# Last output rows by single PSUM banks on three DMA queues, with a new order of all steps

## The chip, the cores and the metric

The kernel runs on one core of a Trainium2 chip. The metric is device time in microseconds; a kernel's time is the median of its runs. The core's engines are TensorE (PE, with its weight loads as PEld), VectorE (DVE), ScalarE (ACT), GpSimd (POOL) and SyncE (SP). Each works through its own instructions in order and waits on semaphores of the others. TensorE writes to PSUM, whose eight banks hold 512 float32 values per partition; ScalarE and VectorE empty them. Transfers run on 16 shared DMA engines and are issued here from POOL (loads) and SP (transposes, output).

## The reference: linear attention into a gated long convolution

For 8 batches of 576 positions, 8 heads of 64 make a model width of 512. All inputs and the output are float32.

```python
kv  = einsum('bhsd,bhse->bhde', k, v)
out = einsum('bhsd,bhde->bhse', q, kv)
out = out / sqrt(mean(out * out, -1) + 1e-6) * g_norm
x   = out.transpose(0, 2, 1, 3).reshape(8, 576, 512)

x1, x2, x3 = split(x @ w_proj, 3, axis=-1)           # w_proj is 512 x 1536
conv = irfft(rfft(x2, axis=1) * rfft(filter, axis=0))   # circular, length 576
return (x1 * conv * x3) @ w_out                       # 512 x 512
```

## The kernel before: a written-out order of small steps

Matrix products run in bfloat16 with float32 sums. The program is one long list of steps, `ORDER`. A word such as `Ga2.0` names a step (`Ga2`) and its batch (0). The loop at the end calls the steps one after another, each of which appends its instructions to the queues of the engines. Nothing is planned at run time: `ORDER` alone decides what stands ahead of what on each engine. A third number, as in `T0.0.19`, asks for so many *fillers* before the step: matmuls of `nil` by `ind`, constants made at the start, into the PSUM bank that the step has just taken. Their results are never read. `take` hands out PSUM banks by the order too, a pair or a single bank, the longest free first.

The names of the steps, by batch:

- `Lq`, `Lk`, `Lv` (halves with `a`, `b`) load q, k, v from POOL's queue, cast to bfloat16 on the way; `Lf` loads the filter, `Lw1`, `Lw2`, `Lw3` the thirds of w_proj, `Lwo` w_out.
- `T0`, `T1` with `eT…` transpose q on TensorE (batches 0 and 1; later `Qt`, by DMA, with `Qh`).
- `K` multiplies k by v, `eK` copies the result; `O` multiplies by q; `sq`, `R`, `rs`, `ob` or `ov`, `x` make the normalisation (square, sum over a head, reciprocal root, scale by g, product).
- `eo`, `fr`, `fa` fold x; `rrM`, `rrT`, `abM`, `abT` project the folded rows to x2; `err`, `eab`, `eT` evict; `F0`, `F1t`, `F1`, `F2c`, `F2` transform; `M0`, `M1`, `M2` multiply with the filter's spectrum; `A0`, `A1` add on POOL (`Av0`, `Av1` on VectorE).
- `Io`, `I` transform back, `oa`, `ov`, `ea`, `ev` evict (a on ScalarE, v on VectorE); `vB`, `w` recombine, `fin` (or `f0`, `f1` by halves) multiplies with the gates.
- `Ga`, `Gb` project to x1 and x3 for one of four column groups; `x1j` (or `xv`) evicts the first, `g` multiplies the second with it.
- `U0`, `U2` multiply two groups of 128 rows with w_out into two banks, `U4` one group that joins the end of an even batch and the begin of the next; `ot…` evicts on ScalarE and sends from SP's queue. `V0` to `V3` do one group of 128 rows into one bank; `va`, `vv` evict and `ds`, `dg` send. `send` cuts a tile at multiples of 96 rows, so a group of 128 rows goes out as two transfers.
- At the start, `Z…` steps make constants, `Ad`, `As`, `Ab`, `Ac` the cosine and sine tables, `Tb`, `et`, `ec` transpose them; `Rv`, `er`, `ff`, `H`, `hv`, `hs`, `Hv`/`HN` make the filter's spectrum.

The start runs: loads on POOL; on TensorE 19 fillers, then q's transposes, more fillers, tables, filter, K.0, O.0 and the first gates (`Ga2.0`). The end runs: the gates of batch 7, the last inverse transforms, the last recombination on VectorE, then `U2.6`, `U2.7`, `V0.7`, `V1.7`, `U4.7` on TensorE, evictions on ScalarE, and sends on SP with one on POOL.

Of the kernel before, what the change touches and what calls it, by code (L numbers as in the profile page):

```python
# [23 lines left out]
sq3.0 ob3.0 Lw2.0 R3.0 hs0.0 x0.0 hv2.0 rs3.0 R2.0 T1.1 rs2.0 ob2.0 x1.0 T0.1 eTa0.1 Lkb.2 Lq.2 hs2.0 Ga2.0.1 Ga3.0
Gb2.0 eTa1.1 Hv1.0 Gb3.0 eo.0 fr.0 x13.0 x12.0 Lq.3 Lka.2 K.1 eK.1 g2.0 Ga1.0 O01.1 g3.0 HN0.0 sq0.1 rrM.0 Lv.2 x11.0
fa1.0 rrT.0 sq1.1 ob1.1 fa0.0 ob0.1 verr.0 abM.0 eab.0 F0.0 abT.0.1 F2c.0 eT.0 O23.1 M0.0 F2.0 sq2.1 Gb1.0 ob2.1 sq3.1
F1t.0 M2.0 A0.0 F1.0 Qt.3 g1.0 ob3.1 R1.1 Ga0.0.1 rs1.1 M1.0 Av1.0 R0.1 R2.1 rs0.1 rs2.1 R3.1 Gb0.0 rs3.1 x.1 Io01.0
eo.1 x10.0 Io23.0 oa01.0 K.2 I01.0 oa23.0 ea01.0 Ga1.1 fr.1 eK.2 Ga0.1 x11.1 Qt.2 I23.0 rrM.1 g0.0 ea23.0 rrT.1 x10.1
err.1 fa.1 O01.2 sq0.2 abT.1 abM.1 sq1.2 vB.0 w.0 ob0.2 f001.0 ob1.2 f101.0 veT.1 eab.1 Gb1.1 O23.2 sq2.2 F0.1 g1.1
ob2.2 Qh.3 Ga3.1 f123.0 f023.0 Gb0.1 sq3.2 ob3.2 R1.2 x13.1 F2c.1 M0.1 rs1.2 g0.1 F2.1 Lk.3 R3.2 F1t.1 rs3.2 Lv.3 R2.2  # L30
rs2.2 M2.1 F1.1 K.3 eK.3 Lqb.4 M1.1 R0.2 Lwo.0 Ga2.1 rs0.2 Gb2.1 O23.3 x12.1 x.2 sq2.3 g2.1 Av1.1 Lv.4 U0.0 sq3.3 R3.3
Lqa.4 Lka.4 Lkb.4 A0.1 ob2.3 eo.2 ob3.3 Gb3.1 Lq.5 rs3.3 ot0.0 I01.1 ea01.1 g3.1 fa0.2 Ga0.2 x10.2 Io23.1 Io01.1
oa23.1 fa1.2 abT.2 I23.1 oa01.1 eT.2 ea23.1 O01.3 fr.2 sq1.3 abM.2 sq0.3 ob1.3 vB.1 Qt.5 w.1 Qt.4 rrM.2 rrT.2 fin.1
eab.2 F1t.2 err.2 K.4 F1.2 Ga3.2 eK.4 ob0.3 x13.2 Gb0.2 R1.3 Gb3.2 rs1.3 M1.2 F0.2 R2.3 g0.2 Ga2.2 g3.2 R0.3 rs2.3
Ga1.2 x12.2 M0.2 rs0.3 x11.2 U4.1 F2c.2 O23.4 A1.2 F2.2 ot4.1 x.3 sq3.4 ob3.4 M2.2 Av0.2 sq2.4 U2.0 ob2.4 Gb2.2 Io01.2
I23.2 ot2.0 g2.2 oa01.2 eo0.3 eo1.3 fa0.3 Qh.5 I01.2 ea23.2 Io23.2 ea01.2 fr.3 R3.4 U0.1 Gb1.2 rs3.4 oa23.2 fa1.3
ot0.1 g1.2 O01.4 sq0.4 vB.2 abT.3 sq1.4 abM.3 Lk.5 eT.3 Lv.5 Lq.6 ob0.4 Lv.6 rrM.3 w.2 f023.2 rrT.3 eab.3 ob1.4 f001.2
F2c.3 K.5 F1t.3 F2.3 F1.3 verr.3 eK.5 R2.4 Ga1.3 Lk.6 M2.3 U2.1 rs2.4 M1.3 f123.2 x11.3 F0.3 ot2.1 R0.4 Ga2.3 rs0.4
R1.4 x12.3 Gb2.3 M0.3 rs1.4 g2.3 x.4 Lv.7 Ga0.3 O23.5 x10.3 sq2.5 sq3.5 ob3.5 f101.2 Gb1.3 U0.2 ob2.5 g1.3 ot0.2 Ga3.3
x13.3 Av0.3 Qt.6 A1.3 eo.4 I01.3 fa0.4 fa1.4 Io23.3 Io01.3 oa23.3 Gb3.3 ea01.3 g3.3 fr.4 I23.3 K.6 oa01.3 O01.5 ea23.3  # L40
eK.6 sq1.5 sq0.5 Gb0.3 g0.3 ob1.5 ob0.5 abM.4 R2.5 rrM.4 vB.3 w001.3 w101.3 abT.4 w023.3 w123.3 fin.3 eab.4 rs2.5 Qh.6
R1.5 eT.4 rrT.4 F1t.4 rs1.5 err.4 F1.4 R0.5 Ga2.4 rs0.5 x12.4 M1.4 Gb2.4 R3.5 F0.4 A1.4 g2.4 Lk.7 rs3.5 M0.4 U2.2 x.5
U4a.3 U4b.3 A0.4 O23.6 F2c.4 ot2.2 F2.4 sq3.6 ot4.3 sq2.6 ov3.6 M2.4 U0.3 eo.5 Ga0.4 ob2.6 ot0.3 I01.4 x10.4 Io01.4
oa01.4 fr.5 Io23.4 oa23.4 Ga3.4 ev01.4 I23.4 ea23.4 x13.4 Lqa.7 Lqb.7 Qt.7 Qh.7 Gb3.4 vB01.4 rrM.5 O01.6 g3.4 sq1.6
vB23.4 ob1.6 rrT.5 verr.5 Gb0.4 g0.4 Ga1.4 x11.4 Gb1.4 R3.6 Ga1.5 sq0.6 ob0.6 fa.5 R2.6 g1.4 rs3.6 F0.5 w.4 rs2.6
abT.5 eT.5 abM.5 x11.5 fin.4 eab.5 M0.5 R1.6 Gb1.5 rs1.6 K.7 F1t.5 g1.5 F2c.5 eKv.7 F2.5 M2.5 R0.6 F1.5 A0.5 rs0.6
M1.5 U2.3 ot2.3 Ga3.5 A1.5 x13.5 Gb3.5 O23.7 x.6 U0.4 sq2.7 g3.5 sq3.7 ov3.7 eo.6 Ga0.5 ob2.7 ot0.4 I23.5 Io23.5 x10.5
Io01.5 Gb0.5 ov23.5 oa01.5 ev23.5 I01.5 ea01.5 fa.6 g0.5 R2.7 Ga2.5 rs2.7 x12.5 abM.6 vB.5 abT.6 O01.7 eab.6 eT.6
Gb2.5 sq0.7 ob0.7 fr.6 w.5 rrM.6 sq1.7 g2.5 rrT.6 fin.5 F2c.6 ob1.7 F1t.6 F2.6 R1.7 err.6 M2.6 F1.6 U0.5 rs1.7 ot0.5
F0.6 Ga1.6 M1.6 R3.7 U2.5 x11.6 R0.7 M0.6 rs3.7 Ga2.6 U2.4 Av0.6 rs0.7 x0.7 A1.6 ot2.5 Gb2.6 x1.7 Io01.6 x12.6 eo.7  # L50
Gb1.6 g2.6 ot2.4 g1.6 Ga0.6 Io23.6 Gb0.6 oa01.6 oa23.6 I23.6 x10.6 I01.6 fa.7 ea23.6 ea01.6 abM.7 abT.7 Ga3.6 fr1.7
g0.6 eab.7 fr0.7 Gb3.6 vB.6 w.6 eT.7 rrM.7 x13.6 F2c.7 g3.6 rrT.7 F1t.7 F1.7 Ga0.7 err.7 fin.6 F2.7 F0.7 U4.5 M1.7
Ga1.7 x10.7 U0.6 x11.7 Gb1.7 M0.7 ot0.6 M2.7 Gb0.7 ot4.5 g1.7 A1.7 A0.7 g0.7 I01.7 Io01.7 Ga2.7 Io23.7 oa01.7 ev01.7
I23.7 oa23.7 Gb2.7 ea23.7 x12.7 Ga3.7 Gb3.7 vB01.7 vB23.7 g2.7 U2.6 w101.7 x13.7 ot2.6 g3.7 f101.7 w123.7 f123.7 U2.7
w023.7 ot2.7 w001.7 f023.7 f001.7 V0.7 V1a.7 V1b.7 U4.7 va1.7 va0.7 ds0.7 va4.7 dg1.7 ds4.7"""


@with_exitstack
def kernel(
# [697 lines left out]

    def send(q, b, at, ot):  # L760

        for i, x in enumerate([ot] if len(ot.shape) == 2 else [ot[:, 0], ot[:, 1]]):
            at_, p = at + i * P, 0
            while p < P:
# [1 line left out]
                q.dma_start(out=o_rows(b, at_ + p, n), in_=x[p:p + n])
                p += n

    def o_rows(b, at, n):
        b, a, c, p = b + at // S, at % S // TH, at % TH // 96, at % 96  # L770
        return bass.AP(tensor=out.tensor, offset=out.offset + (b * S + 6 * p + 2 * c + a) * DM, ap=[[6 * DM, n], [1, DM]])
# [11 lines left out]
            for dc in range(NDC):  # L783
                nc.tensor.matmul(pp[:, cc], ygt(b)[:, dc, b % 2 * 64 + c * P:b % 2 * 64 + (c + 1) * P], wo[:, dc], start=(dc == 0), stop=(dc == NDC - 1))  # L784

    def U_ev(b, c0, ev=act.copy):
        ot = ot_tile()
        ev(out=ot, in_=tmp['u', b, c0])  # L788
        free(("u", b, c0))
        send(nc.sync, b, b % 2 * 64 + c0 * P, ot)  # L790

    def U4(b, d0, d1):
# [2 lines left out]
        for dc in range(d0, d1):  # L795
            nc.tensor.matmul(tmp['u4', b], yg4()[:, b // 2 % 2, dc, 4 * P:5 * P], wo[:, dc], start=(dc == 0), stop=(dc == NDC - 1))
# [13 lines left out]
    step["ot4"] = U4_ev  # L810
    step["ov4r"] = lambda b: U4_ev(b, vec.tensor_copy)


# [12 lines left out]
        ev(out=ot, in_=tmp[k_])  # L826
# [54 lines left out]
```

## Time and profile before

| | |
|---|---|
| median of 3 runs | 215.01 us (214.27 to 215.26) |
| the profiled execution | 214.02 us |
| its span, from the first to the last instruction of the program | 212.2 us |
| TensorE busy | 200.7 us (95%) in 2014 matmuls |
| VectorE busy | 183.1 us (86%) |
| ScalarE busy | 145.8 us (69%) |
| GpSimd busy | 58.8 us (28%) |
| read from, written to HBM | 33.69 MB, 9.44 MB |

The profile is one execution. Times in its rows count from the start of the span. A busy TensorE counts overlapping stretches of pipelined matmuls: one matmul of 512 columns is shown as some 0.38 us, while the next can start 0.22 us after it. A row of the timeline gives start, length, engine, line, operation, what it writes and reads, the number of instructions merged, and in brackets an idle time before it with what ended it. A row "DMA to landing" is from the issue of a transfer to its semaphore.

### The profile page before, as it was taken

To read this page: it belongs to the slowest core of one execution; us is meant where nothing else is said; L and a number is where in the kernel's file an instruction comes from. 1 tells how busy PE (TensorE), PEld (TensorE's weight loads), DVE (VectorE), ACT (ScalarE), POOL (GpSimd) and SP (SyncE) were. 2 spreads that over 40 slices of the span, in tenths; PEclk is the share of its full clock that TensorE was granted. 3 is DMA by queue.
4 is the path that set the end of the run, shared out by engine and by line. 5 is a ranking of instruction groups with operands and counts; after the bars stand their busy time and mean duration, and the time that the engine had idled before them with its cause. 6 is when DMAs were issued, how large, how long until landed. Compare 5 with 4: busy or idle time off the path is not lost.

```text
span 212.2 us, 4930 instructions
## 1 busy us (share of the span) xinstructions
PE 200.7 (95%) x2014; PEld 120.8 (57%) x2014; DVE 183.1 (86%) x285; ACT 145.8 (69%) x240; POOL 58.8 (28%) x64
## 2 busy tenths in 40 slices
...
GB/s 29 200 205 206 207 207 205 204 173 174 203 203 204 204 127 107 181 248 251 213 127 153 60 3 152 285 83 64 99 102 0 34 127 140 3 2 110 38 169 179
DMA packets 37145, 30.14 MB, mean 142 GB/s; under 512 B 15906, under 2 KB 32290, under 8 KB 37122
## 3 DMA queue, kind: packets, MB, share of 16 engines
...
q14 instruction: 8, 0.07, 0.1%
HBM read 33.69 MB, written 9.44 MB: 203 GB/s over the span
## 4 chain that ended last, share of the span: by engine, by line
PE 90%; DVE 3%; ACT 2%; issue 1%; POOL 1%; POOLq 0%; DVEq 0%
PE ps L689 29%; PE ps L784 12%; PE ps L601 7%; PE ps L112 6%; PE ps L718 5%; PE ps L515 3%; PE ps L587 3%; PE ps L607 3%; PE ps L436 3%; PE ps L508 3%; DVE tpw L664 2%; PE ps L594 2%; PE ps L645 2%; PE ps L631 2%; PE ps L373 1%; PE ps L719 1%
## 5 line engine op out<-in xcount | busy, mean ns | idle before, releaser
L689 PE MATMUL ps<-x,wp 128*128 128x288 bf16 x512 | 70.6, 286 | 0.1
L689 PEld LDWEIGHTS <-wp 128*128 128x128 bf16 x512 | 49.1, 98 | 16.7 <-issue 1.6
L670 POOL TENSOR_TENSOR Y<-tpw 128x1024 bf16<-128x1024 f32 (+1 forms) x11 | 28.0, 2549 | 73.5 <-DVE tpw L664 73.5
L664 DVE TENSOR_TENSOR tpw<-ps,HH 97x2048 f32<-97x2048 f32 (+1 forms) x16 | 36.4, 2286 | 2.3 <-PE ps L631 1.8
L784 PE MATMUL ps<-wo,yg 128*128 128x512 bf16 x120 | 28.4, 379 | 0.0
L697 DVE TENSOR_TENSOR g<-ps,x 128x576 bf16<-128x576 f32 x32 | 24.0, 754 | 5.1 <-PE ps L689 3.2
L695 ACT CAST x<-ps 128x576 bf16<-128x576 f32 x32 | 20.4, 641 | 9.3 <-PE ps L689 9.0
L528 ACT ACTIVATE rstd<-ps 128x576 bf16<-128x576 f32 x32 | 20.7, 656 | 7.2 <-PE ps L515 6.7
L788 ACT COPY ot<-ps 128x1024 f32<-128x1024 f32 x15 | 15.2, 1015 | 11.1 <-PE ps L784 11.0
L722 ACT CAST ar<-ps 128x576 bf16<-128x576 f32 x28 | 17.1, 645 | 7.9 <-PE ps L719 7.7
L611 ACT CAST x<-ps 128x1024 bf16<-128x1024 f32 (+1 forms) x20 | 17.2, 869 | 7.6 <-PE ps L601 3.3
L518 ACT ACTIVATE sq<-ps 128x576 bf16<-128x576 f32 x32 | 20.1, 654 | 3.4 <-PE ps L508 3.1
L524 ACT ACTIVATE o<-ps,g_col 128x576 bf16<-128x576 f32 x29 | 21.1, 750 | 0.0
L784 PEld LDWEIGHTS <-yg 128*128 128x128 bf16 x120 | 11.5, 98 | 12.9 <-issue 0.7
L112 PE MATMUL ps<-nil,ind 128*128 128x512 bf16 x42 | 13.9, 453 | 3.5 <-DVE ind L191 3.2
L718 PE MATMUL ps<-IV,Y 128*128 128x192 bf16 x128 | 15.7, 245 | 0.0
L601 PE MATMUL ps<-wp,ab 128*128 128x512 bf16 x64 | 15.1, 379 | 0.0
L515 PE MATMUL ps<-sq,ind 128*128 128x288 bf16 x64 | 12.9, 286 | 0.7 <-DVE tpw L664 0.5
L719 PE MATMUL ps<-IV,Y 97*128 97x96 bf16 x64 | 13.2, 207 | 0.0
L558 DVE TENSOR_TENSOR eo<-x 128x1152 bf16<-128x1152 bf16 (+1 forms) x18 | 12.2, 724 | 0.1
L742 DVE TENSOR_TENSOR yg<-w,g 128x576 bf16<-128x576 bf16 (+1 forms) x17 | 11.9, 718 | 0.2
...
## 6 DMA issues: line engine op xcount, KB each, us to landing
...
vb<-in_v_dram POOLq DMA_DIRECT2D x7, 576.0 KB, 12.5
qb<-in_q_dram POOLq DMA_DIRECT2D x5, 576.0 KB, 13.4
...
kb<-in_k_dram POOLq DMA_DIRECT2D x6, 288.0 KB, 14.0
wp<-in_moe_w_proj_dram POOLq DMA_DIRECT2D x3, 512.0 KB, 17.0
```

The source lines that it names most:

```text
L112: nc.tensor.matmul(pair[i][:, j], ind, nil, start=True, stop=True)
L518: act.activation(out=halves(sq()[:, j]), in_=tmp['o', b, j][:, :, 0:TH], func=AF.Square)
L524: act.activation(out=halves(osb()[:, j]), in_=tmp['o', b, j][:, :, 0:TH], func=AF.Copy, scale=g_col)
L528: act.activation(out=halves(rstd()[:, j]), in_=tmp['r', b, j][:, :, 0:TH], func=AF.Abs_reciprocal_sqrt, scale=1.0 / D, bias=1e-6)
L601: nc.tensor.matmul(pp[:, h], abt()[:, j, 2 * h * P:(2 * h + 1) * P], w2(j), start=(j == 0), stop=(j == NDC - 1))
L664: vec.tensor_mul(out=t_[:n], in0=xp[:n].unsqueeze(1).to_broadcast([n, 2, 2, DM]), in1=two)
L670: op(out=Yt()[:n, 2 * g:2 * g + 2], in0=t_[:n, ::-1, 0], in1=t_[:n, ::-1, 1])
L689: nc.tensor.matmul(pp[:, h, 0:TH], w_, x[:, j, h * TH:(h + 1) * TH], start=(j == 0), stop=(j == NDC - 1))
L695: ev0(out=x1, in_=pp[:, :, 0:TH])
L697: vec.tensor_mul(out=halves(g13t()[:, dc]), in0=pp[:, :, 0:TH], in1=x1)
L718: nc.tensor.matmul(pp[:, i, 0:SB], Y[:, 2 * g + h, cs], IV[:, 2 * g + h, 0:SB], start=(g == 1), stop=(g == 2))
L784: nc.tensor.matmul(pp[:, cc], ygt(b)[:, dc, b % 2 * 64 + c * P:b % 2 * 64 + (c + 1) * P], wo[:, dc], start=(dc == 0), stop=(dc == NDC - 1))
```

## The change

Three things are changed.

First, `send` takes a list of queues and deals the transfers of a tile out to them in turn. New step names use it: `op` (SP and POOL) and `og` (POOL) beside `ot`; `oh` for a single bank of `V` evicted on ScalarE and sent by SP and POOL; `d` with two letters for the last rows (`dag`: first piece on ScalarE's queue, second on POOL's; `dsg`, `das` likewise).

Second, the last rows are computed by single banks: `U2.6` becomes `V2.6` and `V3.6`, `U2.7` becomes `V2.7` (in two halves) and `V3.7`. Each is evicted and sent by itself, four of the last five on VectorE (`vv`).

Third, `ORDER` is written anew from end to end. The filter (`Lf`) is loaded first, before v, q, k of batch 0. The 42 fillers in 14 places become 36 in 6, of which 22 stand in one row ahead of `Rv2.0`. Some loads are cut in halves or joined, and some steps move between ScalarE and VectorE: four evictions of x2 (`verr`, `veT`) and two of the inverse transform move to ScalarE, five more scalings by g (`ov`) and three first gates (`xv`) to VectorE. `A0.2` and `A0.3` are now on POOL, `Av0.7` on VectorE.

The steps `Rq`, `rsw`, `xp` are defined too, but no word of the new `ORDER` calls them.

```diff
-ORDER = """Zj.0 Zi.0 Zf.0 Zk.0 Lqa.0 Z.0 Zt.0 Zd.0 Ad2.0 Zr.0 Lf.0 Zc.0 As2.0 Ad0.0 Ad1.0 Zp.0 Ab2.0 Zh.0 T0.0.19 Ac2.0 Rv01.0.6
-Ab1.0 Lva.0 Lvb.0 Lka.0 As0.0 As1.0 Abv0.0 Lkb.0 Ac0.0 Lq.1 Lqb.0 Tb2.0.1 Rv2.0.1 Ac1.0 erv01.0 era2.0 etv2.0 eTv0.0
-eca2.0 Tb1.0 Act.0 etv1.0 Tb0.0.4 etv0.0 ff0.0 eca1.0 ecv0.0 Lw1.0 Lk.1 Ka.0 eKaa.0 Kb.0.1 O01.0.2 eKb.0 sq1.0 ff1.0
...
-I23.7 oa23.7 Gb2.7 ea23.7 x12.7 Ga3.7 Gb3.7 vB01.7 vB23.7 g2.7 U2.6 w101.7 x13.7 ot2.6 g3.7 f101.7 w123.7 f123.7 U2.7
-w023.7 ot2.7 w001.7 f023.7 f001.7 V0.7 V1a.7 V1b.7 U4.7 va1.7 va0.7 ds0.7 va4.7 dg1.7 ds4.7"""
+ORDER = """Zi.0 Zj.0 Zc.0 Lf.0 Z.0 Zk.0 Zp.0 Zf.0 Zt.0 Zd.0 Zr.0 Ad12.0 Ad0.0 Ab12.0 Rv2.0.22 Rv01.0 Lva.0 Lqa.0 Lka.0 Ac2.0
+Ac1.0 As12.0 As0.0 Tb2.0 Tb1.0 era2.0 era01.0 Abv0.0 Zh.0 T0.0.5 etv2.0 Ac0.0 etv1.0 eca2.0 ff0.0 eTv0.0 Lqb.0 Lvb.0
+Tb0.0 etv0.0 Lqa.1 Lqb.1 ecv0.0 Ka.0 Act.0 eKa.0 O01.0.3 sq1.0 T1.0.1 sq0.0 ecv1.0 ob1.0 ff1.0 H1.0 R0.0 eTv1.0 hv1.0
+Lkb.0 Lw3.0 ob0.0 rs0.0 R1.0 H2.0 rs1.0 Lw1.0 hs1.0 x0.0 Kb.0.2 eKab.0 hv2.0 O23.0 Lkb.1 hs2.0 sq2.0 H0.0 ob2.0 Lka.1
+sq3.0 ob3.0 Lv.1 R2.0 R3.0 rs3.0 rs2.0 T1.1 Lw2.0 Lqb.3 T0.1 eTa1.1 x1.0 Ga2.0 Gb2.0 eo0.0 eTv0.1 eo1.0 Gb0.0.3 Lva.2
+x12.0 Lk.2 g2.0 ha0.0 Lqa.3 Ga0.0 x10.0 Lvb.2 K.1 hs0.0 fr.0 g0.0 Ga1.0 eK.1 x11.0 fa0.0 O01.1 O2.1 rrM.0 fa1.0 sq0.1
...
+oa23.6 ea01.6 Io01.6 oa01.6 fa.7 Gb3.6 x13.6 abT.7 g0.6 eT.7 abM.7 rrM.7 rrT.7 eab.7 F2c.7 F1t.7 F1.7 g3.6 vB.6 Ga3.7
+err.7 x13.7 Ga0.7 w.6 x10.7 Gb3.7 F2.7 F0.7 fin.6 M1.7 U0.6 A1.7 M2.7 U0.5 op0.6 M0.7 og0.5 Gb0.7 Av0.7 g3.7 Io01.7
+I01.7 g0.7 Ga1.7 ea01.7 Gb1.7 x11.7 I23.7 U4a.5 ov01.7 Io23.7 U4b.5 vB01.7 ea23.7 V2.6 oa23.7 g1.7 w101.7 f101.7
+vB23.7 Ga2.7 w123.7 ot4.5 w001.7 oh2.6 Gb2.7 x12.7 g2.7 f123.7 w023.7 V3.6 V2a.7 f001.7 V2b.7 oh3.6 f023.7 va2.7 da2.7
+V3.7 V0.7 U4.7 vv3.7 vv0.7 dag3.7 vv4.7 dag0.7 dsg4.7 V1.7 vv1.7 das1.7"""
...
-    def send(q, b, at, ot):
+    def send(qs, b, at, ot):
+        k = 0
         for i, x in enumerate([ot] if len(ot.shape) == 2 else [ot[:, 0], ot[:, 1]]):
             at_, p = at + i * P, 0
             while p < P:
                 n = min(P - p, 96 - (at_ + p) % 96)
-                q.dma_start(out=o_rows(b, at_ + p, n), in_=x[p:p + n])
+                qs[k % len(qs)].dma_start(out=o_rows(b, at_ + p, n), in_=x[p:p + n])
+                k += 1
                 p += n
...
+        step["op%d" % c0] = lambda b, c0=c0: U_ev(b, c0, qs=(nc.sync, nc.gpsimd))
+        step["og%d" % c0] = lambda b, c0=c0: U_ev(b, c0, qs=(nc.gpsimd,))
...
+    def V_row(b, c, qs):
+        ot = ot_tile()
+        act.copy(out=ot[:, 0], in_=tmp['v', b, c])
+        free(("v", b, c))
+        send(qs, b, b % 2 * 64 + c * P, ot[:, 0])
+
+    for c in range(4):
+        for e, qs in (("s", (nc.sync,)), ("c", (nc.sync, nc.scalar)), ("h", (nc.sync, nc.gpsimd))):
+            step["o%s%d" % (e, c)] = lambda b, c=c, qs=qs: V_row(b, c, qs)
...
-        for e, q_ in (("s", nc.sync), ("g", nc.gpsimd), ("a", nc.scalar)):
-            step["d%s%d" % (e, c)] = lambda b, c=c, q_=q_: V_out(b, c, q_)
+        queues = {"s": nc.sync, "g": nc.gpsimd, "a": nc.scalar}
+        for e in ("s", "g", "a", "sg", "gs", "sa", "as", "ga", "ag"):
+            step["d%s%d" % (e, c)] = lambda b, c=c, e=e: V_out(b, c, [queues[x] for x in e])
```

More of the change, by code (lines that the diff above doesn't have):

```diff
@@ L24 @@
[L24 to L53, printed above, removed]
@@ new lines @@
+x.1 Gb3.0 Io01.0 eK.2 Qh.3 Io23.0 I01.0 oa01.0 Ga0.1 oa23.0 x10.1 eo.1 Ga1.1 Lk.3 ea01.0 I23.0 fr.1 fa0.1 ea23.0 g3.0
+rrM.1 fa1.1 rrT.1 x11.1 abT.1 err.1 Lva.3 vB.0 O01.2 eT.1 Lvb.3 sq1.2 w.0 sq0.2 f001.0 abM.1 ob0.2 Lwo.0 ob1.2 Gb0.1
+f101.0 eab.1 F0.1 O23.2 Lk.4 sq2.2 g0.1 ob2.2 M0.1 f023.0 sq3.2 Gb1.1 ob3.2 g1.1 Ga2.1 R2.2 Lq.4 F2c.1 F2.1 x12.1 R3.2
+K.3 rs2.2 rs3.2 M2.1 x1.2 F1t.1 F1.1 R0.2 Ga3.1 eK.3 rs0.2 x13.1 M1.1 f123.0 Av1.1 R1.2 Gb2.1 Lva.4 O23.3 rs1.2 sq2.3
+ob2.3 g2.1 x0.2 Lvb.4 U0.0 A0.1 Io01.1 Lqa.5 Io23.1 Lqb.5 sq3.3 ob3.3 eo.2 Ga2.2 oa01.1 oa23.1 x12.2 I01.1 Gb3.1
@@ new lines @@
+ea01.1 I23.1 fa.2 g3.1 ot0.0 abT.2 ea23.1 O01.3 eT.2 sq1.3 fr.2 abM.2 sq0.3 rrM.2 ob1.3 R1.3 eab.2 rrT.2 Qt.5 rs1.3
+K.4 ob0.3 err.2 F1t.2 vB.1 F1.2 eK.4 Gb2.2 Ga1.2 w.1 Qt.4 fin.1 x11.2 M1.2 g2.2 Gb1.2 R0.3 Ga0.2 g1.2 F0.2 rs0.3 xv0.2
+R3.3 U4a.1 A1.2 Qh.5 rs3.3 U4b.1 R2.3 Lka.5 Lkb.5 Lv.5 Ga3.2 F2c.2 M0.2 rs2.3 x.3 O23.4 F2.2 x13.2 sq2.4 ov2.4 A0.2
+M2.2 sq3.4 U0.1 ob3.4 op4.1 og0.1 Gb0.2 eo1.3 U2.0 g0.2 I01.2 I23.2 eo0.3 fa.3 ot2.0 ea01.2 Gb3.2 Io01.2 ea23.2 Io23.2
+g3.2 oa01.2 Lv.6 abT.3 oa23.2 K.5 fr.3 Lk.6 eT.3 O01.4 vB.2 eK.5 w.2 abM.3 sq0.4 rrM.3 Lq.6 ob0.4 F1t.3 Lq.7 rrT.3
@@ new lines @@
+eab.3 F2c.3 fin.2 sq1.4 ob1.4 F2.3 F1.3 U2.1 M2.3 err.3 ot2.1 M1.3 F0.3 Ga0.3 R3.4 rs3.4 x10.3 Ga3.3 A1.3 Gb3.3 x13.3
+M0.3 R0.4 g3.3 rs0.4 R2.4 Gb0.3 g0.3 R1.4 Ga1.3 A0.3 I01.3 rs2.4 rs1.4 Ga2.3 x11.3 O23.5 ea01.3 U0.2 x12.3 Gb2.3 sq2.5
+Lk.7 x.4 sq3.5 ob2.5 eo.4 fa.4 I23.3 ov3.5 ot0.2 Io23.3 Io01.3 g2.3 fr.4 Qt.6 ea23.3 oa23.3 abT.4 oa01.3 O01.5 abM.4
+eT.4 sq1.5 ob1.5 vB.3 R1.5 sq0.5 rs1.5 ob0.5 w.3 eab.4 Gb1.3 g1.3 rrM.4 rrT.4 F1t.4 err.4 fin.3 K.6 F1.4 Ga2.4 R2.5
+eKm.6 x12.4 Gb2.4 F0.4 M1.4 rs2.5 Qt.7 g2.4 R0.5 rs0.5 R3.5 U2.2 rs3.5 A1.4 M0.4 F2c.4 O23.6 U4.3 F2.4 x.5 A0.4 op2.2
@@ new lines @@
+Ga0.4 sq2.6 ot4.3 sq3.6 ov2.6 x10.4 M2.4 U0.3 I23.4 eo0.5 eo1.5 Io01.4 Qh.7 ob3.6 ot0.3 oa01.4 ea23.4 Ga1.4 fr.5 I01.4
+ea01.4 Io23.4 Lv.7 xv1.4 rrM.5 O01.6 oa23.4 rrT.5 fa.5 sq0.6 Gb0.4 vB.4 ob0.6 err.5 Gb1.4 g0.4 sq1.6 g1.4 w.4 ob1.6
+Ga3.4 Ga2.5 x13.4 R0.6 xv2.5 Gb3.4 rs0.6 g3.4 R3.6 F0.5 R1.6 rs1.6 abM.5 rs3.6 fin.4 eab.5 abT.5 eT.5 Gb2.5 R2.6 M0.5
+K.7 A0.5 rs2.6 F1t.5 F2c.5 x0.6 eK.7 F1.5 g2.5 M1.5 F2.5 M2.5 Ga3.5 U2.3 x13.5 Gb3.5 O23.7 ot2.3 U0.4 sq3.7 g3.5 Ga0.5
+A1.5 x1.6 sq2.7 ob3.7 ov2.7 og0.4 Io23.5 Ga1.5 Io01.5 oa23.5 x10.5 I23.5 x11.5 Gb0.5 I01.5 oa01.5 eo.6 fa.6 fr.6
```

40 lines of the change are left out of this document (33 added, 7 removed).

## The prediction, made blind

> **What bounds the kernel now.** I read the page's shares first, then the chain of waits, then the engines by stretches of time, then the two ends in order of time.
>
> ```profile
> PE 200.7 (95%) x2014; PEld 120.8 (57%) x2014; DVE 183.1 (86%) x285; ACT 145.8 (69%) x240; POOL 58.8 (28%) x64
> ...
> PE 90%; DVE 3%; ACT 2%; issue 1%; POOL 1%; POOLq 0%; DVEq 0%
> ...
> 28.00:50.00 22.00, 21.03 (x293) 13.20 (x292) 19.06 (x24) 16.80 (x28) 5.86 (x7) 1.00 1.26 202
> 50.00:203.00 153.00, 152.93 (x1477) 94.28 (x1475) 143.22 (x200) 109.51 (x174) 38.51 (x30) 1.00 0.65 125
> ```
>
> The columns are the stretch, its length, and the busy time of PE, PEld, DVE, ACT and POOL, then clock, DMA share and GB/s. TensorE carries nine tenths of the chain, and from 50 to 203 us it is idle 0.07 us in 153, at clock 1.00. VectorE comes next: from 28 to 203 us it is idle 2.94 + 9.78 = 12.7 us of 175. So between the ends time falls only with TensorE's own work; a new order can add a stall there, hardly remove one. What is left are the start and the end.
>
> The start, in order of time; the two landing rows are those of vb and of wp (min/median/max from issue to landing):
>
> ```profile
> 12.89 0.74 POOL L142 DMA_DIRECT2D vb<-in_v_dram x1 [0.69 <-DMA vb<-in_v_dram]
> DMA to landing us min/median/max: 6.6/11.8/19.3
> 14.36 0.74 POOL L150 DMA_DIRECT2D wp<-in_moe_w_proj_dram x1 [0.73 <-DMA kb<-in_k_dram]
> DMA to landing us min/median/max: 14.0/17.0/19.9
> 16.43 0.48 PE L436 MATMUL ps<-vb,kb 64*64 64x64 bf16 x36
> 23.22 0.44 PE L508 MATMUL ps<-qT,kvblk 64*64 64x288 bf16 x8
> 27.99 4.17 PE L689 MATMUL ps<-x,wp 128*128 128x288 bf16 x32
> 30.00:32.30 2.30, 2.17 (x21) 1.53 (x20) 2.23 (x5) 1.18 (x2) 0.48 (x1) 1.00 1.24 208
> 32.29 0.77 PE L436 MATMUL ps<-vb,kb 64*64 64x64 bf16 x72
> 34.69 1.04 PE L587 MATMUL ps<-wp,rr 128*128 128x512 bf16 x4
> ```
>
> The v rows of batch 1 are issued at 12.89 and land 19.3 us later, at 32.2; the matmuls on them (L436, step K.1) start at 32.29. The last third of w_proj lands at 14.36 + 19.9 = 34.3, and the first matmul that reads it (L587, rrM.0) starts at 34.69. The DMA engines are full at that time (208 GB/s, share 1.24). So the data set the start, and what TensorE does before 32.2 waits for them in the end.
>
> The end, in order of time, with the rates of the DMA engines in three of its microseconds, and last the landing times of all rows of the output:
>
> ```profile
> 196.18 3.10 PE L689 MATMUL ps<-x,wp 128*128 128x288 bf16 x24
> 199.12 3.78 PE L784 MATMUL ps<-wo,yg 128*128 128x512 bf16 x16
> 202.90 1.90 PE L820 MATMUL ps<-wo,yg 128*128 128x512 bf16 x8
> 204.64 1.03 PE L796 MATMUL ps<-wo,yg 128*128 128x512 bf16 x4
> 204.84 1.07 ACT L826 COPY kb<-ps 128x512 f32<-128x512 f32 x2 [0.90 <-PE ps L820]
> 205.72 1.06 POOL L766 DMA_DIRECT2D out_dram<-kb  x2 [12.26 <-ACT kb L826]
> 205.80 0.60 ACT L826 COPY sq<-ps 128x512 f32<-128x512 f32 x1
> 206.34 1.05 SPq L766 DMA_DIRECT2D out_dram<-kb  x2
> 207.49 1.25 SPq L766 DMA_DIRECT2D out_dram<-sq  x2
> 205.00:206.00 1.00, 0.66 (x4) 0.10 (x1) 0.00 (x0) 1.00 (x3) 0.28 (x1) 1.00 0.81 197
> 207.00:208.00 1.00, 0.00 (x0) 0.00 (x0) 0.00 (x0) 0.00 (x0) 0.00 (x0) 1.00 1.02 311
> 211.00:212.20 1.20, 0.00 (x0) 0.00 (x0) 0.00 (x0) 0.00 (x0) 0.00 (x0) 0.50 0.00 0
> DMA to landing us min/median/max: 1.6/2.8/7.2
> ```
>
> TensorE's last matmul (L796) ends at 205.67, so 6.5 us of the 212.2 follow it. ScalarE has the last tile at 206.40, but SyncE, with two issues of the kb rows from 206.34 on, begins on it only at 207.49. Data move until about 211, and the last microsecond holds nothing. Of the 6.5 us, 0.7 is the eviction, 1.1 the wait for SyncE, and the rest two issues in a row, the landing and the finish.
>
> **The change part by part.**
>
> *Fillers.* 42 matmuls on constants become 36.
>
> ```profile
> 38.60 0.38 PE L112 MATMUL ps<-nil,ind 128*128 128x512 bf16 x1
> 38.82 1.03 PE L607 MATMUL ps<-wp,ab 128*128 128x512 bf16 x4
> 43.32 0.38 PE L112 MATMUL ps<-nil,ind 128*128 128x512 bf16 x1
> ```
>
> Only two of the 42 lie behind K.1, and from its start to the next matmul's one takes 38.82 - 38.60 = 0.22. Both go: -0.4. The other four that go, and the earlier begin of the row of 22 (its operands are now written before the angle columns), lie before data that land at the same time: 0; without that cover they would be worth 0.9.
>
> *Order of the loads.* What precedes v of batch 1 in the queue is the same set as before (filter, q, k, v of batch 0, q and k of batch 1, two thirds of w_proj), so it lands at 32.2 again, and the last third of w_proj at 34.3. Splitting loads adds POOL issues of 0.74 each, hidden by a queue that the data fill 19 us ahead. The filter's path (Rv, ff, H) moves ahead of the q transposes, the second half of k behind q of batch 1: 864 KB more stand before it (the second half of q of batch 0 and q of batch 1), at 208 GB/s 4.3 us. So Kb.0 moves from 16.43 to 20.7; with its three copies (about 1 us) O23.0 comes at 22 to 22.5, where it stands at 23.22 now. From O23.0 to the first gate 27.99 - 23.22 = 4.8 us pass, so that gate starts near 27. Four gates at 0.98 (196.18 to 199.12 are three) and three fillers at 0.22 end at 31.6: cover of 0.6 us. Value 0; bounds -0.3 (the first DMA, a third of the filter, is shorter) and +1.0 (third rival).
>
> *Engines exchanged in the middle.*
>
> ```profile
> L616 DVE CAST x<-ps 128x1024 bf16<-128x1024 f32 (+1 forms) x4 | 4.3, 1086 | 1.2 <-PE ps L594 1.2
> L522 DVE TENSOR_SCALAR o<-ps,g_col 128x576 bf16<-128x576 f32 x3 | 2.4, 814 | 0.2
> L670 DVE TENSOR_TENSOR Y<-tpw 97x1024 bf16<-97x1024 f32 (+1 forms) x5 | 6.2, 1232 | 0.1
> L391 DVE TENSOR_SCALAR hu<-ps,pc 128x512 f32<-128x512 f32 x2 | 1.4, 743 | 0.0
> ```
>
> VectorE loses four L616 casts (-4.3), two ar evictions (L391 as the nearest row, 0.743: -1.5) and one L670 sum (-1.2). It gains five scalings by g (5 x 0.814 = 4.1), three first gates and four last rows (7 x 0.743 = 5.2). Its smaller exchanges (transposes, k-v copies, the filter's scaling and turning) I put at -1 together. Sum +1.3 us, beside 12.7 us idle: 0 by itself. ScalarE gets the reverse and has more room (idle 43 us of the 153). Some 25 pieces of output go from SP to POOL, at 0.53 each 13 us on an engine idle 114 us of the 153; behind them stand loads and sums that their readers need later: 0. A stall in the middle I bound by -0.6 (stalls between 28 and 50 that go; later none is there to go) and +3, and take 0.
>
> *The end on TensorE.* Before, 28 output matmuls follow the last gate; now 24, with V2.6 ahead of it: the same work. VectorE's order beside it changes.
>
> ```profile
> 179.06 1.89 PE L601 MATMUL ps<-wp,ab 128*128 128x512 bf16 x8
> 180.05 0.56 DVE L729 TENSOR_TENSOR vt<-ar 128x768 bf16<-128x768 bf16 x1
> 182.72 0.75 DVE L739 TENSOR_TENSOR w<-bb 128x1152 bf16<-128x1152 bf16 x1
> 184.67 1.36 DVE L742 TENSOR_TENSOR yg<-w,g 128x2304 bf16<-128x2304 bf16 x1
> 186.12 1.14 PE L689 MATMUL ps<-x,wp 128*128 128x288 bf16 x8
> 186.39 4.49 DVE L664 TENSOR_TENSOR tpw<-ps,HH 128x2048 f32<-128x2048 f32 x2 [0.36 <-PE ps L645]
> ```
>
> Now VectorE waits for F1.7 (0.36 us) before its products. TensorE needs 186.12 - 179.06 = 7.1 us from abM.7 through F1.7, two gates (1.96) among them, which the new order puts elsewhere: 5.1. Beside that VectorE has two g (0.75 each), vB.6 and w.6 (180.05 to 183.47: 3.4) and fin.6 (1.4): 6.3, so it is 1.2 late. Then come 4.5 for the products, 1.2 for M2.7 (a float result of the L670 kind) and 1.2 for the sum Av0.7 (on VectorE now, was POOL's): 8.1 us after F1.7 Io01.7 may start. TensorE covers 8.3: four gates 3.9, F2 and F0 4 x 0.22, U0.6 and U0.5 at 1.74 each (202.90 to 204.64 is eight matmuls). Behind the last gate V3.6 and V2a.7 (1.3) cover g2.7 and f123.7 (0.75, 0.46 and two handovers): 0.2 is left open. Stalls that go: 16 output matmuls took 3.78 where twice 1.74 is 3.48, so -0.3. Sum 0, within -0.3 and +3.
>
> *The end after TensorE.* Each output bank is evicted alone and its pieces go to two queues. After V1.7: eviction on VectorE 0.77 with its handover, then a free queue (POOL now starts 0.3 after half of the 1.07 of the two evictions; SP could start at once), landing 1.6 to 3.2, last microsecond 1.0. No row shows a DMA issued by ScalarE; between 0 and 0.3 I take 0.1, as SP is the nearer, and the median 2.8 for the landing. Sum 4.7, against 6.5: -1.8; bounds 3.4 (-3.1) and 6.3 (-0.2, first rival).
>
> **Sum.** -0.4 + 0 + 0 + 0 - 1.8 = -2.2. The profiled execution took 214.02 us for a span of 212.2, so 1.8 lie around it; the median of the runs, 215.01, is 1.0 above it. The span should be near 210.0 and the median 215.01 - 2.2 = 212.8.
>
> **The rivals.**
>
> *The output drains no sooner.* Six banks of 262 KB follow the last gate. V3.6's lies ready 3.7 us before TensorE's end (five groups at 0.87, less 0.60 for its eviction). At 311 GB/s the six take 5.1 us and are done 1.4 us after TensorE, earlier than the last piece can land. At 197 GB/s they take 8.0, until 4.3 after; with 1 us to land and 1 to finish 6.3, as now. For it: shares of 0.81 to 1.02 in these rows. Against: 311 is what the engines did once the queue was full. Time 215.01 - 0.4 - 0.2 = 214.4. [...]
>
> *VectorE becomes the bound at the end (slower).* Each microsecond that it is late at fin.6 beyond the 0.2 to spare goes straight through Av0.7 to Io01.7. From 2.2 + 1.1 + 0.2 = 3.5 us of extra lateness on, the gain has become a loss of over half a per cent. VectorE's load (143.2 of 153 us) makes lost leads of 4 to 5 us possible: 212.8 + 4.3 = 217.1. Against: it waits for TensorE there now.
>
> *The start slips.* Should O23.0 come 1.6 us later than I count, K.1 is 1 us late, and the early VectorE work before rrM.0 with it: 213.8.
>
> **How the numbers follow.** Forecast 0.59, drain 0.18, late VectorE 0.13, start 0.10. The first gives 211.3 to 213.9 by its bounds. Half a per cent is about what a measurement of this kernel tells from no change: 213.93 to 216.09. Of the forecast's cases 0.04 and nearly all of drain fall within it, of start 0.05, and of late VectorE none below 216.09 but 0.01; so faster 0.60, same 0.27, slower 0.13. The range leaves out some 0.06 at the fast end and most of late VectorE: 211.2 to 215.6.
>
> **What would show it.** Right: K.1 again at 32.2 to 32.5 and rrM.0 near 34.7; TensorE without idle from 50 us on; its last matmul at 205 to 206; then 4.2 to 5.2 us to the span's end, with no SyncE issue more than 0.5 us behind its eviction. Wrong: first gates after 28.5; TensorE idle for VectorE's tpw, Y or yg by more than 2 us in sum; or DMA shares near 1 until the last microsecond.

## The result, and the profile after

The median falls from 214.64 us (213.98 to 215.26, 4 runs beside it) to 211.84 us (211.55 to 213.06): a ratio of 0.9882, 95% interval 0.9845 to 0.9919. The profiled execution took 211.77 us for a span of 210.0 us, against 214.02 and 212.2.

The page of the kernel after, its busy times and its chain:

```profile
PE 199.2 (95%) x2008; PEld 120.4 (57%) x2008; DVE 182.5 (87%) x280; ACT 142.5 (68%) x233; POOL 76.5 (36%) x92
...
PE 84%; DVE 11%; ACT 2%; issue 1%; DVEq 0%; ACTq 0%
```

TensorE still carries the chain, with 1.5 us less busy time and six matmuls fewer (the fillers); VectorE's share of the chain rises from 3% to 11%. POOL has 17.7 us more, mostly the 24 more output pieces that it now sends and one sum more. The two middle stretches (columns as before: stretch, length, PE, PEld, DVE, ACT, POOL, clock, DMA share, GB/s):

```profile
28.00:50.00 22.00, 21.53 (x300) 13.82 (x299) 20.61 (x31) 15.91 (x28) 4.95 (x6) 1.00 1.28 194
50.00:203.00 153.00, 152.84 (x1470) 93.89 (x1469) 141.30 (x187) 109.19 (x172) 55.31 (x57) 1.00 0.67 130
```

From 50 to 203 us TensorE is idle 0.16 us, where it was 0.07 before. By this view nothing changed there; from 28 to 50 us its idle time falls from 0.97 to 0.47 us. The start and the end in order of time, TensorE and the queues of the last rows:

```profile
2.06 7.82 PE L112 MATMUL ps<-nil,ind 128*128 128x512 bf16 x22 [2.06 <-DVE ind L191]
20.83 0.48 PE L436 MATMUL ps<-vb,kb 64*64 64x64 bf16 x36
26.53 2.42 PE L715 MATMUL ps<-x,wp 128*128 128x288 bf16 x16
31.49 0.78 PE L436 MATMUL ps<-vb,kb 64*64 64x64 bf16 x72
34.19 1.02 PE L613 MATMUL ps<-wp,rr 128*128 128x512 bf16 x4
...
198.02 3.91 PE L851 MATMUL ps<-wo,yg 128*128 128x512 bf16 x16
199.60 1.84 PEld L851 LDWEIGHTS <-yg 128*128 128x128 bf16 x10 [0.61 <-DVE yg L768]
201.77 1.03 PE L824 MATMUL ps<-wo,yg 128*128 128x512 bf16 x4
202.63 1.03 PE L851 MATMUL ps<-wo,yg 128*128 128x512 bf16 x4
203.70 0.69 DVE L857 COPY kb<-ps 128x512 f32<-128x512 f32 x1 [0.17 <-PE ps L851]
203.82 0.54 POOL L793 DMA_DIRECT2D out_dram<-sq  x1 [0.35 <-DVE sq L857]
204.42 0.31 SPq L793 DMA_DIRECT2D out_dram<-kb  x1
```

Kb.0 comes at 20.83 (forecast 20.7), the first gate at 26.53 (27), K.1 at 31.49 (32.2 to 32.5), rrM.0 at 34.19 (34.7). TensorE ends at 202.63 + 1.03 = 203.66. From there 6.3 us remain to 210.0; before they were 6.57. SyncE now takes the last tile 0.03 us after its eviction (203.70 + 0.69 to 204.42) where it was 1.1 late. But the transfer does not land sooner. The DMA engines in these microseconds, and the landing times of SyncE's two issues after 203.4:

```profile
203.00:204.00 1.00, 0.66 (x4) 0.10 (x1) 0.83 (x2) 0.00 (x0) 0.65 (x2) 1.00 0.99 244
204.00:205.00 1.00, 0.00 (x0) 0.00 (x0) 0.39 (x1) 0.00 (x0) 0.36 (x1) 1.00 0.85 275
205.00:206.00 1.00, 0.00 (x0) 0.00 (x0) 0.00 (x0) 0.00 (x0) 0.00 (x0) 0.96 0.93 248
206.00:207.00 1.00, 0.00 (x0) 0.00 (x0) 0.00 (x0) 0.00 (x0) 0.00 (x0) 0.50 0.86 236
207.00:208.00 1.00, 0.00 (x0) 0.00 (x0) 0.00 (x0) 0.00 (x0) 0.00 (x0) 0.50 0.34 125
DMA to landing us min/median/max: 3.7/3.9/4.1
```

The shares are 0.85 to 0.99 for four microseconds, at 236 to 275 GB/s: the engines are occupied nearly all the time. SyncE's last piece takes 3.7 us from issue to landing; ScalarE's piece of the same bank, also issued at 204.42, takes 3.9 and lands last, at 208.35.

So by the two profiles 2.2 us of span went: 0.5 from rrM.0's start, 1.50 from the stretch between rrM.0 and TensorE's end (205.66 - 34.69 = 170.97; now 203.66 - 34.19 = 169.47), 0.23 from what follows. The experiments ask which of these three is the change and which is the one execution.

### The profile page after: what moved, and what is told of

It is laid out like the page before. It is cut to its first block, busy times and chain, and to the rows that moved or that the text cites. A ratio compares the mean times of both kernels' runs of the same rounds, so it can differ in the third digit from the quotient of the medians.

```text
span 210.0 us, 4918 instructions
## 1 busy us (share of the span) xinstructions
PE 199.2 (95%) x2008; PEld 120.4 (57%) x2008; DVE 182.5 (87%) x280; ACT 142.5 (68%) x233; POOL 76.5 (36%) x92
## 4 chain that ended last, share of the span: by engine, by line
PE 84%; DVE 11%; ACT 2%; issue 1%; DVEq 0%; ACTq 0%
PE ps L715 27%; PE ps L812 11%; PE ps L627 7%; PE ps L112 5%; PE ps L744 4%; PE ps L613 3%; PE ps L515 3%; PE ps L633 3%; PE ps L508 2%; PE ps L620 2%; DVE tpw L690 2%; PE ps L436 2%; PE ps L851 2%; PE ps L671 2%; PE ps L824 2%; PE ps L657 2%
## 5 line engine op out<-in xcount | busy, mean ns | idle before, releaser
L696 POOL TENSOR_TENSOR Y<-tpw 97x1024 bf16<-97x1024 f32 (+1 forms) x12 | 30.9, 2580 | 88.9 <-DVE tpw L690 88.9
L721 ACT CAST x<-ps 128x576 bf16<-128x576 f32 x29 | 18.3, 640 | 10.4 <-PE ps L715 9.7
L812 PE MATMUL ps<-wo,yg 128*128 128x512 bf16 x104 | 24.4, 380 | 0.0
L637 ACT CAST x<-ps 128x1024 bf16<-128x1024 f32 (+1 forms) x24 | 20.8, 875 | 5.3 <-PE ps L627 3.6
L816 ACT COPY ot<-ps 128x1024 f32<-128x1024 f32 x13 | 13.2, 1016 | 10.2 <-PE ps L812 10.2
L793 POOL DMA_DIRECT2D out_dram<-ot x23 | 12.0, 524 | 16.9 <-ACT ot L816 9.7
L541 ACT ACTIVATE o<-ps,g_col 128x576 bf16<-128x576 f32 x24 | 17.7, 747 | 0.0
L112 PE MATMUL ps<-nil,ind 128*128 128x512 bf16 x36 | 11.7, 477 | 2.1 <-DVE ind L191 2.1
L569 DVE TENSOR_TENSOR x<-o,rstd 128x1152 bf16<-128x1152 bf16 (+1 forms) x11 | 11.3, 1024 | 2.3 <-ACT rstd L550 2.1
L584 DVE TENSOR_TENSOR eo<-x 128x576 bf16<-128x576 bf16 (+1 forms) x22 | 12.1, 593 | 0.1
```

Of the source, the lines that this page charges most:

```text
L112: nc.tensor.matmul(pair[i][:, j], ind, nil, start=True, stop=True)
L637: act.copy(out=o_(), in_=tmp[key, b])
L696: op(out=Yt()[:n, 2 * g:2 * g + 2], in0=t_[:n, ::-1, 0], in1=t_[:n, ::-1, 1])
```

## The experiments

**The kernel after once more,** in five rounds, as the measure for the others.

> The new kernel once more, beside the others of this job, as their reference. By every theory 2.3 to 2.8 us below before. Its first gate may come at another time than 26.53 us: in three profiles that share its start it came at 25.9, 27.0 and 27.2, the two late ones with a granted TensorE clock of 0.5 for 3.4 us between 22.6 and 27.8. If the clock gate is what scatters the start, a late first gate goes with such a stretch here too, and an early one without.

211.91 us, 0.9879 [0.9861, 0.9897]; 2.6 us below the 214.48 of the kernel before. rrM.0 comes at 34.30, the stretch to TensorE's end is 169.48 us, and 6.15 us stand behind it. Its first gate comes at 25.87 with no fall of the clock, as expected; but the late gate of the first profile (26.53) has no fall of the clock either, so the clock is not all that scatters the start.

**The new end alone, and everything but the new end.** The first is the old order up to `U2.6` with the new last rows; the second the new order up to the last batch with the old last rows.

```diff
 (new end alone: the old ORDER, from U2.6 on)
-U2.6 w101.7 x13.7 ot2.6 g3.7 ... U2.7 w023.7 ot2.7 ... V1a.7 V1b.7 U4.7 va1.7 va0.7 ds0.7 va4.7 dg1.7 ds4.7
+V2.6 V3.6 w101.7 x13.7 oh2.6 oh3.6 g3.7 ... V2.7 V3.7 ... da2.7 ... vv3.7 vv0.7 dag3.7 vv4.7 dag0.7 dsg4.7 V1.7 vv1.7 das1.7
 (old end: the new ORDER, from ea23.7 on)
-V2.6 oa23.7 g1.7 ... oh2.6 ... V3.6 V2a.7 f001.7 V2b.7 oh3.6 f023.7 va2.7 da2.7 V3.7 ... das1.7
+oa23.7 g1.7 ... U2.6 f123.7 w023.7 ot2.6 U2.7 f001.7 ot2.7 f023.7 V0.7 V1a.7 V1b.7 U4.7 va1.7 va0.7 ds0.7 va4.7 dg1.7 ds4.7
```

> The old order, but from U2.6 on with the new tail: V2.6, V3.6, V2.7, V3.7, V0.7, U4.7, V1.7 bank by bank, evicted and sent on three queues as in the new kernel. Theory A (the prediction's term): what follows TensorE's end shrinks from 6.5 to 4.7 us, so 1.8 us faster than before. Rival B (the output drains at the rate of the DMA engines): what follows TensorE's end stays above 6 us, so 0 to 0.5 us faster than before.

> The new order up to U4b.5, then the old tail: U2.6 and U2.7 by pairs of banks, V0.7, V1.7, U4.7, evictions on ScalarE, sends on SP and one on POOL. Theory A: the new kernel loses its 1.8 us here and stands 0.4 to 0.7 us below before. Rival B: it stays within 0.5 us of the new kernel, 2.3 to 2.8 us below before.

New end alone: 213.62 us, ratio 0.9959 [0.9941, 0.9977]. Old end: 212.62 us, 0.9927 [0.9901, 0.9952]. Both times the result stands between the two theories. Of the 2.6 us the end is worth 0.9 (or 214.4 x (0.9927 - 0.9879) = 1.0, from the other side), and the rest of the order 1.6. The stretch from rrM.0 to TensorE's end shows where that 1.6 lies: it is 170.97 us with the old order and the new end, 169.18 with the new order and the old end. With the old order the new end moves nothing on TensorE; with the new order it costs 0.3 us there (169.47 against 169.18). It shortens what follows: 5.84 to 6.34 us in the five profiles with the new end that change nothing else behind it, 6.57 to 6.94 in the four with the old one; means 6.13 and 6.77, so 0.64. By the spans, which leave out what lies around them, the end is worth less from the other side: the median is 210.3 us with the old end and 209.95 in the eight executions of the kernel after, so 0.35, which is 0.64 less those 0.3. The runs leave the end's worth between 0.4 and 1.0 us.

**The new start alone.** The new order up to rrM.0, then the old order.

> The new order up to rrM.0 (with column group 3 in place of 0 in its third and fourth gate), then the old order, old tail and old queues. Theory P (both starts wait for the same data, the last third of w_proj at 33.8): rrM.0 at 34.1 to 34.8 as in the old order, the rest 170.8 to 171.2 us long as there, so within 0.5 us of before. Rival: the new start is worth 0.5 us or more, 0.5 to 1 us faster than before.

214.95 us, 1.0013 [0.9992, 1.0035]: no difference. Its TensorE row next to that of the new end alone, which has the old start:

```profile
34.15 1.02 PE L613 MATMUL ps<-wp,rr 128*128 128x512 bf16 x3
```

```profile
34.13 1.04 PE L614 MATMUL ps<-wp,rr 128*128 128x512 bf16 x3
```

The first gates come at 26.03 and 27.63, and rrM.0 at the same time, 0.3 us after w_proj's last third has landed (33.88 and 33.81). In the profile of before that third landed at 34.25. With the old start rrM.0 stands at 34.13, 34.53 and 34.69 in three profiles, with the new one at 34.01 to 34.30 where the clock held and the row of 22 stands (means 34.45 and 34.18); if the new start helps by 0.2 or 0.3 us, the times don't show it. The time of this run can't settle it: its stretch from rrM.0 is 171.76 us, 0.6 above what theory P allowed, with a wait of 0.67 us for ScalarE at 35.7, just behind the place where the two orders join.

**Halving the last rows.** Is the end limited by the engines that move it? Each of the last five banks sends only half of its rows; the other half of these rows is left out of the output.

```diff
-                qs[k % len(qs)].dma_start(out=o_rows(b, at_ + p, n), in_=x[p:p + n])
+                qs[k % len(qs)].dma_start(out=o_rows(b, at_ + p, n // part), in_=x[p:p + n // part])
...
-        send(qs, *((b - 1, 4 * P) if key == 4 else (b, b % 2 * 64 + key * P)), tmp['ot', b, key])
+        send(qs, *((b - 1, 4 * P) if key == 4 else (b, b % 2 * 64 + key * P)), tmp['ot', b, key], 2)
```

> The new kernel, but each transfer of the last five banks (V2.7, V3.7, V0.7, U4.7, V1.7) sends only the first half of its rows; the other half is left out, 655 KB less. Rival B: at 250 GB/s the data end up to 2.6 us earlier, then the landing time of a single transfer (1.6 to 2.8 us after its issue at about 204.4) sets the end: span 1.0 to 2.2 us shorter than the new kernel's. Theory A (issue and landing of the last piece set the end): within 0.3 us of the new kernel.

210.36 us, 0.9811 [0.9786, 0.9836]: 1.5 us faster than the kernel after. What follows TensorE falls from 6.34 to 4.38 us, as rival B had it (the last row is of SyncE's two issues again):

```profile
203.00:204.00 1.00, 0.95 (x5) 0.29 (x3) 0.82 (x2) 0.00 (x0) 0.58 (x2) 1.00 0.57 131
204.00:205.00 1.00, 0.13 (x1) 0.00 (x0) 0.69 (x1) 0.00 (x0) 0.51 (x1) 1.00 0.74 205
205.00:206.00 1.00, 0.00 (x0) 0.00 (x0) 0.00 (x0) 0.00 (x0) 0.00 (x0) 1.00 0.61 146
206.00:207.00 1.00, 0.00 (x0) 0.00 (x0) 0.00 (x0) 0.00 (x0) 0.00 (x0) 1.00 0.29 94
DMA to landing us min/median/max: 1.6/1.6/1.6
```

SyncE's last issue (204.89, 0.76 after TensorE's end as before) lands 1.6 us later instead of 3.7, ScalarE's beside it, the last to land, 2.0 later instead of 3.9. So some 2 us of the new end are bytes of these rows in the DMA engines: bytes queued ahead of the last piece, and its own, which this run doesn't tell apart. (In this profile the start was 0.5 us late, with a fall of the clock that is told of at the end.)

**Two queues, and one.** First POOL's sends at the end go to SyncE and ScalarE; then SyncE sends all of the last rows.

```diff
-oh2.6 ... oh3.6 ... da2.7 ... dag3.7 ... dag0.7 dsg4.7 ... das1.7
+oc2.6 ... oc3.6 ... da2.7 ... das3.7 ... das0.7 dsa4.7 ... das1.7    (two)
+os2.6 ... os3.6 ... ds2.7 ... ds3.7 ... ds0.7 ds4.7 ... ds1.7    (one)
```

> The new kernel, but the pieces of the last banks (V2.6, V3.6, V3.7, V0.7, U4.7) that went to POOL's queue go to ScalarE's. In the new kernel's profile POOL's closing drain ends 0.6 us after the last landing and SyncE waits for it; before, it ended 1.0 us ahead of the last landing. Theory C (POOL's drain closes the span): 0.4 to 0.6 us shorter than the new kernel. Rival (only the data count): within 0.2 us of it, or up to 0.3 us longer, as ScalarE's queue issues more pieces in a row.

> The new kernel with all pieces of the last seven banks on SP's queue. Theory B (drain): ten pieces at 0.31 to 0.6 us each from 200.9 on keep SP issuing until about 206; the data are late by what the queue is late at the end, 0.5 to 1.2 us slower than the new kernel. Rival (the issue is hidden by the drain, and POOL's closing drain is gone): within 0.3 us of the new kernel.

Two queues: 211.58 us, 0.988 [0.9852, 0.9908]; one: 211.45 us, 0.986 [0.9841, 0.9878]; the kernel after, measured beside the latter, 211.91. Three queues bring nothing over one that shows; the slowing by 0.5 to 1.2 us that theory B gave for one queue didn't come. With one, SyncE's last issue is at 206.30, 1.9 us later than with three, and the last byte lands at 208.29, as with three (208.35):

```profile
204.51 1.12 SPq L793 DMA_DIRECT2D out_dram<-sq  x2
205.73 1.00 SPq L793 DMA_DIRECT2D out_dram<-kb  x2
DMA to landing us min/median/max: 2.0/2.3/2.6
```

The later issues land sooner after they are issued (the last 2.0 us, instead of 3.7 to 3.9). So the issue time that three queues saved here was then spent waiting. But a share near 1 is no fixed rate: with two queues the engines moved 352 and 295 GB/s from 205 to 207 us, at shares of 0.98 and 0.90, where they moved 248 and 236 with three. Why isn't shown.

**The row of 22 constants taken away.**

```diff
-Rv2.0.22
+Rv2.0
```

> The new kernel without the row of 22 fillers ahead of Rv2.0. [...] Rival (the row, which ends at 8.3 to 9.7 us, only delays Rv2.0, whose filter has landed at 8.5): same or up to 0.5 us faster.

212.25 us, 0.9897 [0.9872, 0.9922], 0.3 above the kernel after with overlapping intervals. In its profile rrM.0 came at 35.64, 1.4 us late, and the first matmuls on constants that it still has, at 12 us, ran at 0.43 us each:

```profile
11.99 2.31 PE L112 MATMUL ps<-nil,ind 128*128 128x512 bf16 x5
34.82 1.02 PE L613 MATMUL ps<-wp,rr 128*128 128x512 bf16 x3
```

(The second row is the run with two queues, spoken of below.) With the row of 22 that pace doubles at 8.0 us, from 0.43 to 0.22, 5.9 us after the first matmul (2.06). Without it the trace's first record of the full clock stands at 14.7, 6.5 us after the first matmul (8.20): the twelve matmuls of q's transposes at 14.10 take 0.80 us to the next group's start, where in the kernel after they take 0.52 (12.93 to 13.45). (Ahead of that record the views' clock column reads 1.00 all the same, so there the pace has to be read from the starts.) So the row brings TensorE to its speed earlier, at 8.0 instead of 14.7 us. What that is worth differs from one execution to the next: three of the six without the row span 209.8 to 210.1 us, like seven of the eight of the kernel after, and three 210.8 to 211.4, the profiled one among them. The median hides this, and six runs don't settle how often it happens.

**Two fillers less.** The old order without `abT.0.1`'s and `Ga0.0.1`'s constants, the two that stand behind K.1.

> The kernel before, less the two matmuls on constants that stand behind K.1 (at 38.6 and 43.3 us). By their start-to-start time of 0.22 us each TensorE's stretch from rrM.0 to its last matmul falls from 170.97 to 170.54 us and the time from 214.5 to 214.1 (ratio 0.998). Rival: they fill a wait of TensorE for another engine; then the stretch stays at 170.9 to 171.0 and the time at 214.5 (1.000).

214.47 us, 0.9991 [0.9975, 1.0007], and the stretch from rrM.0 is 171.06 us: nothing. The rival's sign is there. Behind the places of the two fillers TensorE waits for VectorE's tpw, 0.28 us where the kernel before shows no wait, and 0.74 where it shows 0.52, together 0.50 more. The first row is the kernel before, the others are this run:

```profile
45.69 0.41 PE L515 MATMUL ps<-sq,ind 128*128 128x288 bf16 x2 [0.52 <-DVE tpw L664]
41.05 1.14 PE L689 MATMUL ps<-x,wp 128*128 128x288 bf16 x8 [0.28 <-DVE tpw L664]
45.52 0.40 PE L515 MATMUL ps<-sq,ind 128*128 128x288 bf16 x2 [0.74 <-DVE tpw L664]
```

**Engines given back.** The new order with eight `ov` as `ob` and three `xv` as `x1`, in place.

```diff
-ov0.1 ov1.1 ov2.1 ov2.4 ov3.5 ov2.6 ov0.7 ov2.7 xv0.2 xv1.4 xv2.5
+ob0.1 ob1.1 ob2.1 ob2.4 ob3.5 ob2.6 ob0.7 ob2.7 x10.2 x11.4 x12.5
```

> The kernel after, with eight evictions of attention rows and three of filter inputs in the middle given back from VectorE to ScalarE, in the same places of the order. If the 0.9 us that TensorE's stretch lost beyond fillers and the moved O2.1 come from the order of the steps, the stretch stays at 169.4 to 169.6 us and the time at 211.7 to 212.1. If they come from the exchanged engines (banks freed sooner), it rises to 170.0 to 170.4 and the time to 212.4 to 212.8.

213.23 us, 0.9937 [0.9916, 0.9958], 1.3 us of the gain gone, and the stretch is 170.90 us, above what either theory gave. Most of it stands in one place:

```profile
127.60 0.74 ACT L541 ACTIVATE o<-ps,g_col 128x576 bf16<-128x576 f32 x1
128.40 1.46 PE L812 MATMUL ps<-wo,yg 128*128 128x512 bf16 x6 [0.88 <-ACT o L541]
```

ScalarE has a double output tile, a square, a single output tile, another square and now the scaling in a row, and TensorE's U2 waits for its bank. In the kernel after, VectorE did that scaling at 125.85, in a gap, and the same U2 began at 126.92. So the exchange doesn't speed up what was there; it keeps out a wait that the new order would have, and without it most of the middle's 1.6 us is gone. The run undoes one side of the exchange alone: what the new order moves to ScalarE (evictions of x2 and of the inverse transform, three other scalings) stays there, so in this stretch ScalarE is busy 126.9 us, against 123.4 in the kernel before. The exchange as a whole wasn't undone.

**One queue with more constants in the start.** One SyncE queue, and eight more fillers between 19 and 24 us (`Kb.0.5`, `O23.0.3`, `R2.0.2`).

> The kernel after with SyncE alone sending the last rows, as in the run with one queue (211.45 us, ratio 0.986), and eight more matmuls on constants between 20 and 24 us, where TensorE waits for other engines. If those waits only let the clock fall now and then, and the data set rrM.0, it starts at 34.1 to 34.3 us again, the clock shows 1.00 from 10 us on, and the time is 211.3 to 211.6. Rival: the added matmuls push the gates behind the landing of v; rrM.0 comes at 34.5 to 35.0 and the time at 211.8 to 212.3.

212.85 us, 0.9906 [0.9876, 0.9937]: no better than the kernel after, and above what either theory gave. The start did as the first theory said (rrM.0 at 34.01, clock 1.00 throughout), and TensorE ended at 203.48, 0.2 us before it does in the kernel after. But a single SyncE issue, the first of these three, took 1.98 us instead of 0.5, with the line standing behind it, and the DMA share fell to 0.05:

```profile
200.67 3.24 SPq L793 DMA_DIRECT2D out_dram<-vb  x3
...
202.00:203.00 1.00, 1.00 (x6) 0.49 (x5) 0.83 (x2) 0.00 (x0) 0.00 (x0) 1.00 0.05 10
```

In this profile that took 1.3 us of the end (last landing at 209.64, against 208.29 with one queue before). Two of the six executions span 209.9 and 210.2 us and the others 210.9 to 212.1; whether a slow issue made these long, too, isn't shown. No version is shown to beat the kernel after while computing all of it.

## Why the prediction was right, and where its steps were not

The total was right (212.8 forecast, 211.84 measured; -2.2 forecast, -2.6 to -2.8 measured), but three of its terms were not. Two gave too much and one too little, and that they nearly cancelled is luck. Most of the signs named for "right" failed, too: K.1 came at 31.49 and TensorE's end at 203.66, both too early, and 6.3 us followed it, not 4.2 to 5.2.

- *Start, 0:* right as far as the runs tell, and for the reason given: rrM.0 stands 0.3 to 0.45 us behind w_proj's landing with either start. That v of batch 1 "lands at 32.2 again" was not so (31.30 in the kernel after); with the old start it landed at 31.27, 31.99 and 32.15.
- *Fillers, -0.4:* the step that failed is "one takes 38.82 - 38.60 = 0.22. Both go". They filled waits for VectorE's tpw; taken out alone they bring nothing (171.06 against 170.97 us; in time at most 0.5 by the interval).
- *Engines exchanged in the middle, 0 with bounds of -0.6 and +3:* the gain was 1.6 us, outside the bounds and the largest of all. Two sentences failed. "A new order can add a stall there, hardly remove one" took 152.93 busy of 153 us for matmuls at full rate. A busy stretch of one matmul is shown as 0.38 us while the next one started 0.22 after it (38.60 and 38.82), so by these figures a start that comes up to 0.16 late leaves no idle time. The rows of the kernel after show it: as little idle from 50 us on (0.16 us), yet the stretch is 1.50 shorter. The second is the price of zero for the exchange "by itself", taken from the sum of VectorE's load beside its idle time: the eleven evictions given back cost 1.2 to 1.3 us, through ScalarE, which I had put down as having room. The sum itself was off as well (VectorE's busy time fell from 183.1 to 182.5, where +1.3 was counted), but it is the place in the order that made the wait. Of the 1.5 us, 0.62 is work (two fillers at 0.22; four matmuls of O2.1, now ahead of rrM.0, at some 0.047 from one start to the next). The fillers count here and not in the run without them, because in the new order no wait for tpw takes their place (its one wait between 36 and 47 us is 0.24, for Y). The remaining 0.9 is spread over many changes from one group of matmuls to the next, and I can't tie it to single steps. Some 0.3 of it was in plain sight: from rrM.0 to 50 us TensorE's idle time falls from 0.67 to 0.35 us, which the bound of -0.6 for stalls between 28 and 50 had allowed for.
- *End on TensorE, 0:* right in sum. VectorE was not the bound: Io01.7 begins without a wait. The 0.2 left open behind the last gate is there, as 0.28 us (PE's stretch from 199.60 on waits for yg). The -0.3 for stalls that go didn't come: 16 output matmuls take 3.91 us, 3.78 before.
- *End after TensorE, -1.8:* that each eviction finds a free queue was right, the term mis-sized; -0.9 to -1.0 measured by the medians, -0.6 by the profiles of this part. Of the eviction, the free queue and the landing the first two came as counted; the landing was taken at 2.8 and is 3.9, and the last microsecond is 1.65 (210.0 - 208.35). With six banks ready sooner the engines are occupied (shares 0.85 to 0.99), and the saved issue time became waiting (the last piece lands 3.7 to 3.9 us after its issue, 2.0 with one queue). That is the rival "the output drains no sooner", in part: its price of 6.3 us after TensorE is what the profile shows (6.3), but the old end costs 6.77 in the mean, not 6.5. Of the signs named, shares near 1 stood until 207, 1.35 us short of the last landing.

Had I set the middle at 0 and the drain at its measured size, the sum would have been 1.3 us, half of what came.
